# A fused attention and token-mixing kernel: units in pairs, quarter-array matmuls, word-wide f16 copies, stores held back

## The chip, the core and the metric

The kernel runs on one core of a Trainium2 chip. Times are device microseconds of one execution. The core has a matrix engine (TensorE, PE in the profile, with its weight loads listed apart as PEld), a vector engine (VectorE, DVE), an activation engine (ScalarE, ACT), a general engine (GpSimd, POOL) and a synchronisation engine (SyncE, SP). Each works through its own queue in order; they meet in semaphores. TensorE writes its results to PSUM, which has 8 banks of 2 KB in each of 128 partitions; VectorE and ScalarE bring them from there to the main on-chip memory (SBUF). Here POOL starts all loads and SP all stores, and 16 DMA engines carry them.

## The reference

Attention inside chunks of 64 tokens, for 8 batches, 8 heads, 576 tokens and 64 numbers a head, and after it, per batch, a token mixer without a softmax:

```python
scores = scale * np.matmul(q_c, k_c.transpose(0, 1, 2, 4, 3))    # per chunk of 64
scores = scores - np.max(scores, axis=-1, keepdims=True)
attn = np.exp(scores)
attn = attn / (np.sum(attn, axis=-1, keepdims=True) + 1e-09)
out = np.matmul(attn, v_c)
# the heads side by side give x: (8, 576, 512); then
wq = x @ w_q                                    # 512 -> 64
wk = x @ w_k
W_tok = scale * np.einsum('bsd,btd->bst', wq, wk)
mixed = np.einsum('bst,btd->bsd', W_tok, x)
return (np.maximum(mixed, 0.0) @ w_out).astype(np.float32)
```

Since nothing nonlinear stands between `W_tok` and `mixed`, the kernels form G = wk^T x first (64 x 512 for a batch) and then `mixed` = wq G.

## The kernel before, in words

**Units.** A unit is 128 tokens of one batch, all 8 heads: two chunks. 576 tokens are four units and 64 tokens over; the left-over tokens of two neighbouring batches make up one "rest" unit. Two batches are thus nine units, 36 in all.

**Loads.** POOL issues them in the order of the units (lines 197 to 212), casting fp32 to f16 on the way. q and k come for two units at a time, with two neighbouring tokens in one partition (line 176); v comes for one unit (line 195). Nothing is reused among these buffers, so no load waits for compute. The weights follow after the third and the fifth unit.

**Stages.** For two units the q and k tiles are turned by matmuls against the identity, with half the array's columns each ("tall", `turn`, line 233), and copied out of PSUM by VectorE (line 314). Then, unit by unit: scores, 16 matmuls of 64x64 in the two diagonal quarters of the array (line 336); their maximum and the subtraction on VectorE (lines 346 and 360); exp on ScalarE (370); the turn of the exponentials by the whole array or its column halves (230, 233) and its copy by ScalarE (381); the product with v and a column of ones, again in the two diagonal quarters (393); the denominators, their reciprocals and the division on VectorE (405 to 408). For two units together: the turn of x (230), its copy by ScalarE (441), the projections (448, 457) and their copy (467). For each batch: G in column halves (493, 502) and its copy (512). Then for two units the mixing in row halves (531) into two banks, the scaled ReLU by ScalarE bank by bank (551), by VectorE for one bank in the last two batches (549), and unit by unit the output product, 4 matmuls of 128x512 (567), its copy (577) and the store on SP (579), at once when the copy is done.

**Order.** Every such step is a `Node` with an engine, a priority, a cost and the nodes that it needs. `plan` (line 41) simulates the four queues before anything is emitted: at each turn it takes, among the nodes of an engine that could start within 0.25 us of the soonest, the one of least priority number (the unit's number plus a lag of the stage, line 277). A change of the array's form (full, tall, wide, quart) counts 0.094 us there. Of the 8 PSUM banks six go round singly and two are held together for the product with v. The engine of each step is fixed beforehand. The instructions are emitted in that order, and each engine runs its own in it.

Of the kernel before, what the change touches and what calls it, by code (L numbers as in the profile page):

```python
# [18 lines left out]
class Node:  # L19


    def __init__(self, eng, prio, busy, emit, deps, forms=(), takes=None, reads=None, tail=0.1):
        self.eng, self.prio, self.busy, self.emit = eng, prio, busy, emit
        self.deps, self.forms, self.tail = deps, forms, tail
        self.form = None
        self.takes = takes or []
        self.reads = reads
        self.done = None
        if reads is not None:
            reads.readers += 1  # L30


class Bank:


    def __init__(self, wide=False):
        self.wide, self.readers = wide, 0
        self.slot, self.left, self.tile, self.end = None, None, None, 0.0


def plan(nodes, ring, wides, switch=0.094, sem=0.06, look=0.25):


    free_at = {("r", i): 0.0 for i in range(ring)} | {("w", i): 0.0 for i in range(wides)}
    held = set()
    users = {}
    waiting = {}
    for n in nodes:
        waiting[n] = len(n.deps)
        for d in n.deps:  # L50
            users.setdefault(d, []).append(n)
    ready = {e: [] for e in ("PE", "DVE", "ACT", "DMA")}
    clock = dict.fromkeys(ready, 0.0)
    form = None
    for n in nodes:
        if not waiting[n]:
            ready[n.eng].append(n)
    order, left = [], len(nodes)

    def start_of(n):  # L60
        at = max([clock[n.eng]] + [d.done + sem for d in n.deps])
        slots = []
        for bk in n.takes:
            kind = "w" if bk.wide else "r"
            free = [(t, k) for k, t in free_at.items() if k[0] == kind and k not in held and k not in slots]
            if not free:
                return None, None
            early = [f for f in free if f[0] + sem <= at]
            t, slot = min(early, key=lambda f: (-f[0], f[1])) if early else min(free)
            at = max(at, t + sem)  # L70
            slots.append(slot)
        if n.eng == "PE" and form is not None and form not in n.forms:
            at = max(at, clock["PE"] + switch)
        return at, slots

    while left:
        best = None
        for e in ready:
            options = []
            for n in ready[e]:  # L80
                at, slot = start_of(n)
                if at is not None:
                    options.append((at, n.prio, n, slot))
            if not options:
                continue
            soonest = min(o[0] for o in options)
            o = min((o for o in options if o[0] <= soonest + look), key=lambda o: (o[1], o[0]))
            if best is None or o[0] < best[0]:
                best = o
        at, _, n, slot = best  # L90
        for bk, sl in zip(n.takes, slot):
            bk.slot, bk.left = sl, bk.readers
            held.add(sl)
        if n.eng == "PE":
            if form not in n.forms:
                form = n.forms[0]
            n.form = form
        clock[n.eng] = at + n.busy
        n.done = at + n.busy + n.tail
        n.at = at  # L100
        if n.reads is not None:
            n.reads.left -= 1
            n.reads.end = max(n.reads.end, n.done)
            if not n.reads.left:
                held.discard(n.reads.slot)
                free_at[n.reads.slot] = n.reads.end
        ready[n.eng].remove(n)
        for u in users.get(n, ()):
            waiting[u] -= 1
            if not waiting[u]:  # L110
                ready[u.eng].append(u)
        order.append(n)
        left -= 1
    return order


@with_exitstack
def kernel(
# [14 lines left out]
    CH, P, R, G = 64, 128, 2, 32  # L133
    NF = DM // P
    NM = S // P
    scale_attn = 1.0 / math.sqrt(D)
    scale_moe = 1.0 / math.sqrt(DH)
    VW = D + 2

# [5 lines left out]


    units, tiles = [], {}
    for b in range(0, B, 2):
        for bb, ms in ((b, range(NM)), (b, [None]), (b + 1, range(NM))):
            for m in ms:  # L150
                units.append((bb, m))
    NU = len(units)

# [6 lines left out]


    def rows(x, b, t0, n):
        return x[b, :, t0 : t0 + n, :].rearrange("h p d -> p h d")

    def pairs(x, b, t0, h0, h1):
        return x[b, h0:h1, t0 : t0 + 2 * P, :].rearrange("h (p r) d -> p h (r d)", r=R)

    qk = {}

    def load_pair(u, heads):  # L170
        b, m = units[u]
        for name, x in (("q", q), ("k", k)):
            qk[name, u] = const.tile([P, H, R * D], F16, name=f"{name}n{u}")
        for h0, h1 in heads:
            for name, x in (("q", q), ("k", k)):
                nc.gpsimd.dma_start(qk[name, u][:, h0:h1, :], pairs(x, b, m * P, h0, h1))  # L176

    def load_rest(u):
        b, _ = units[u]
        for name, x in (("q", q), ("k", k)):  # L180
            qk[name, u] = const.tile([P, H, D], F16, name=f"{name}n{u}")
            for i in range(2):
                nc.gpsimd.dma_start(
                    qk[name, u][CH * i : CH * i + CH, :, :], rows(x, b + i, NM * P, CH)
                )

    def load_v(u):
        b, m = units[u]
        if m is None:
            for i in range(2):  # L190
                nc.gpsimd.dma_start(
                    v_all[CH * i : CH * i + CH, u, :, 0:D], rows(v, b + i, NM * P, CH)
                )
        else:
            nc.gpsimd.dma_start(v_all[:, u, :, 0:D], rows(v, b, m * P, P))  # L195

    for u in range(NU):
        b, m = units[u]
        if m is None:
            load_rest(u)  # L200
        elif m % 2 == 0:
            load_pair(u, [(0, 4), (4, 8)] if u == 0 else [(0, 8)])
# [3 lines left out]
        if u == 2:  # L206
# [4 lines left out]
        if u == 4:  # L211
            nc.gpsimd.dma_start(wo[:], moe_w_out.rearrange("(f p) n -> p f n", p=P))

# [8 lines left out]
    PEd, DVd, ACd = 0.18, 0.09, 0.1  # L222
    FULL, TALL, WIDE, QUART = ("full",), ("tall",), ("wide",), ("quart",)
    EITHER = FULL + TALL

    def turn(form, to, of, i):


        if form == "full":
            nc.tensor.transpose(to, of[:, 2 * i : 2 * i + 2, :], ident[:])  # L230
        else:
            for o in range(2):
                nc.tensor.transpose(to[CH * o : CH * o + CH], of[:, 2 * i + o, :], ident[:])  # L233

    def dve(n, two=1):
        return n / two / 960 + 0.066
# [4 lines left out]
    def bank(tile_of, slot_of):  # L241

        shape, dtype, name = tile_of
        if slot_of.tile is None:
            kind, i = slot_of.slot
            slot_of.tile = psum.tile(shape, dtype, name=name, tag=f"{kind}{i}")
        return slot_of.tile

    arrive = {}
    at = 4.5  # L250
    for u in range(NU):
        b, m = units[u]
        if m is None:
            at += 0.75
        elif m % 2 == 0:
            at += 2.6
            arrive["v", u] = at
        arrive["qk", u] = at
        at += 0.7
        arrive["v", u] = at  # L260

    def landed(key):
        n = Node("DMA", 0, 0.0, lambda: None, [], tail=arrive[key])
        nodes.append(n)
        return n

    PU = 2 * NM + 1
    xs = {}

    def x_of(u):  # L270

        if u // PU not in xs:
            xs[u // PU] = work.tile([P, PU, H, D], F16, name="xs", tag="xs", bufs=2)
        return xs[u // PU][:, u % PU]

    st = {}
    LAG = {"tq": -3.0, "S": 0.0, "mx": 0.0, "E": 1.0, "PV": 1.0, "x": 1.0, "xT": 2.0, "pj": 2.0}

    def transposes(u):

        b, m = units[u]
        pri = u + LAG["tq"]
        there = landed(("qk", u))
        if m is None:
            bk = Bank()

            def pe(form):
                tp = bank(([P, 2, NF, P], F16, "tp"), bk)
                for t, name in enumerate("qk"):
                    for j in range(NF):  # L290
                        turn(form, tp[:, t, j, :], qk[name, u], j)

# [10 lines left out]
        for t, name in enumerate("qk"):  # L303
            bk = Bank()

            def pe(form, bk=bk, name=name):
                tp = bank(([P, NF, 4, R, G], F16, "tp"), bk)
                for j in range(NF):
                    for r in range(R):
                        turn(form, tp[:, j, :, r, :], qk[name, u][:, :, r * D : r * D + D], j)  # L310
# [340 lines left out]
```

## Time and profile before

| | |
|---|---|
| median of 3 runs | 164.35 us (164.33 to 166.39) |
| span of the profiled execution | 163.6 us |
| PE busy | 133.3 us, 81%, 2576 matmuls |
| DVE busy | 111.3 us, 68%, 227 instructions |
| ACT busy | 103.1 us, 63%, 187 instructions |
| POOL busy | 77.4 us, 47% |
| read from and written to memory | 29.75 MB, 9.44 MB |
| granted TensorE clock, mean | 0.986 |

The profiled execution's span runs from its first instruction to its last; the median of the runs is 0.7 us above it. A line of a group or a timeline names the source line, the engine, the operation, the result and its inputs, their shapes (partitions x elements) and a count, then microseconds. Busy time counts a matmul until its result is out, so that matmuls which follow each other overlap in it; how often one can start is read from the starts. The 40 digits of a slice row are tenths of 1/40 of the span. In a table of stretches each engine has its busy time and its number of instructions, then the granted clock, the DMA share and GB/s.

### The profile page before, as it was taken

The page shows a single profiled execution, that of the slowest core. Times are in us where ns is not written, and L with a number is a line of the kernel's source. Part 1 is how long each engine was busy: PE and PEld are TensorE (multiplying, and loading weights), DVE is VectorE, ACT ScalarE, POOL GpSimd, SP SyncE. Part 2 cuts the span into 40 slices and gives each one's busy share as a digit, 9 for nine tenths or more (in the row PEclk, how much of TensorE's full clock was granted, in tenths as well). Part 3 has the DMA queues.
Part 4 walks back from the last instruction along what each step waited for, and adds up shares of the span by engine and source line. Part 5 has one row for each costly group of instructions (what it writes and reads, how often), then busy time and mean ns, then how long its engine had stood idle before and what let it go on. Part 6 is the DMA issues. An engine that isn't in the chain of part 4 may idle for free.

```text
span 163.6 us, 5896 instructions
## 1 busy us (share of the span) xinstructions
PE 133.3 (81%) x2576; PEld 95.3 (58%) x2576; DVE 111.3 (68%) x227; ACT 103.1 (63%) x187; POOL 77.4 (47%) x100
## 2 busy tenths in 40 slices
PE   0447559798899989998999999989989997894870
PEld 0435448576557756775677667856766675553320
DVE  0164545979948947989499489985894899760350
ACT  3012023467798697878977968698779697944510
POOL 7999998674998445598672697000000000000000
PEclk9999999999999999999999999999999999999698
DMA  3999999999999999999999999993300422033053
GB/s 36 126 149 157 137 180 171 171 172 164 130 172 228 241 171 197 242 208 204 170 240 239 164 177 236 205 167 119 148 2 6 165 95 68 0 128 132 0 220 103
DMA packets 86650, 24.70 MB, mean 151 GB/s; under 512 B 81504, under 2 KB 82016, under 8 KB 86624
## 3 DMA queue, kind: packets, MB, share of 16 engines
q0 software_dynamic: 81376, 14.88, 112.2%
q1 hardware_dynamic: 5248, 9.44, 16.6%
q8 instruction: 20, 0.33, 0.8%
q14 instruction: 6, 0.05, 0.1%
HBM read 29.75 MB, written 9.44 MB: 240 GB/s over the span
## 4 chain that ended last, share of the span: by engine, by line
PE 39%; DVE 24%; ACT 15%; POOL 10%; DMA 4%; issue 4%; DVEq 0%; ACTq 0%; POOLq 0%
PE op L567 16%; DVE sh L360 8%; DVE mx L346 6%; DVE xs L408 5%; ACT rm L551 5%; PE xp L393 4%; DMA kn<-in_k_dram 4%; ACT es L370 4%; PE tp L233 3%; PE tx L230 3%; ACT xt L441 3%; PE sp L336 3%; PE pj L448 3%; POOL v_all L195 2%; POOL qn L176 2%
## 5 line engine op out<-in xcount | busy, mean ns | idle before, releaser
L567 PE MATMUL op<-wo,rm 128*128 128x512 f16 x144 | 37.8, 392 | 0.5 <-DVE rm L549 0.5
L370 ACT ACTIVATE es<-sh 128x512 f16<-128x512 f32 x36 | 23.2, 644 | 18.3 <-DVE sh L360 13.1
L381 ACT COPY et<-ep 128x512 f16<-128x512 f16 x36 | 21.7, 602 | 14.7 <-PE ep L233 9.4
L195 POOL DMA_DIRECT2D v_all<-in_v_dram x32 | 28.6, 912 | 1.9 <-DMA v_all<-in_v_dram 1.8
L346 DVE TENSOR_REDUCE mx<-sp 128x8 f32<-128x512 f32 x36 | 24.6, 682 | 2.6 <-PE sp L336 2.5
L408 DVE TENSOR_TENSOR xs<-xp,rec 128x512 f16<-128x512 f32 x36 | 24.9, 691 | 1.2
L577 ACT COPY osb<-op 128x512 f32<-128x512 f32 x31 | 19.0, 612 | 8.0 <-PE op L567 6.7
L360 DVE TENSOR_TENSOR sh<-sp,mx 128x512 f32<-128x512 f32 x32 | 22.1, 689 | 2.6 <-ACT xt L441 0.5
L314 DVE COPY qt<-tp 128x1024 f16<-128x1024 f16 x16 | 11.0, 685 | 16.5 <-PE tp L233 16.5
L551 ACT ACTIVATE rm<-ma 128x512 f16<-128x512 f32 (+1 forms) x35 | 20.3, 683 | 1.4 <-PE ma L531 1.4
L567 PEld LDWEIGHTS <-rm 128*128 128x128 f16 x144 | 13.2, 100 | 13.1 <-issue 2.2
L441 ACT COPY xt<-tx 128x1024 f16<-128x1024 f16 (+1 forms) x20 | 18.7, 934 | 2.7 <-PE tx L230 2.1
L233 PE MATMUL tp<-ident,qn 128*64 128x128 f16 x256 | 11.7, 239 | 9.9 <-POOL ident masks.py:199 5.0
L393 PE MATMUL xp<-v_all,et 64*64 64x65 f16 x576 | 16.8, 198 | 2.2 <-ACT et L381 0.7
L393 PEld LDWEIGHTS <-et 64*64 64x64 f16 x576 | 12.7, 110 | 9.3 <-ACT et L381 6.2
L176 POOL DMA_DIRECT2D kn<-in_k_dram x17 | 15.1, 886 | 5.5 <-DMA kn<-in_k_dram 4.5
L176 POOL DMA_DIRECT2D qn<-in_q_dram x17 | 15.3, 901 | 2.6 <-DMA qn<-in_q_dram 1.1
L314 DVE COPY kt<-tp 128x1024 f16<-128x1024 f16 x16 | 10.9, 683 | 6.5 <-PE tp L233 6.5
L233 PEld LDWEIGHTS <-qn 128*64 128x64 f16 x256 | 8.8, 120 | 11.1 <-DMA qn<-in_q_dram 9.9
L336 PE MATMUL sp<-kt,qt 64*64 64x64 f16 x512 | 13.2, 202 | 0.8 <-DVE kt L314 0.8
L230 PE MATMUL tx<-ident,xs 128*128 128x128 f16 x128 | 9.9, 219 | 4.6 <-ACT rm L551 3.7
L336 PEld LDWEIGHTS <-qt 64*64 64x64 f16 x512 | 11.0, 117 | 2.9 <-issue 1.8
(47 smaller groups left out, 178.8 us busy)
## 6 DMA issues: line engine op xcount, KB each, us to landing
out_dram<-osb SPq DMA_DIRECT2D x32, 256.0 KB, 4.2
v_all<-in_v_dram POOLq DMA_DIRECT2D x32, 128.0 KB, 9.1
qn<-in_q_dram POOLq DMA_DIRECT2D x15, 256.0 KB, 7.9
kn<-in_k_dram POOLq DMA_DIRECT2D x15, 256.0 KB, 8.5
out_dram<-osb SPq DMA_DIRECT2D x8, 128.0 KB, 3.8
qn<-in_q_dram POOLq DMA_DIRECT2D x8, 64.0 KB, 8.4
kn<-in_k_dram POOLq DMA_DIRECT2D x8, 64.0 KB, 6.5
v_all<-in_v_dram POOLq DMA_DIRECT2D x8, 64.0 KB, 4.8
```

What stands on the lines that cost most here:

```text
L176: nc.gpsimd.dma_start(qk[name, u][:, h0:h1, :], pairs(x, b, m * P, h0, h1))
L195: nc.gpsimd.dma_start(v_all[:, u, :, 0:D], rows(v, b, m * P, P))
L233: nc.tensor.transpose(to[CH * o : CH * o + CH], of[:, 2 * i + o, :], ident[:])
L336: nc.tensor.matmul(sp[r, 2 * j + c, :], lhsT=qt[r, j, c * CH : c * CH + CH], rhs=kt[r, j, c * CH : c * CH + CH], start=True, stop=True,)
L346: nc.vector.tensor_reduce(mx[:], bs.tile[:], axis=AX.X, op=ALU.max)
L360: nc.vector.tensor_tensor(out=sh[:].rearrange("p i (g r) -> p i r g", r=R), in0=sp[:].rearrange("p i (r g) -> p i r g", r=R), in1=mx[:, :, ...
L370: nc.scalar.activation(es[:], st["sh", u][:], AF.Exp, scale=scale_attn)
L393: nc.tensor.matmul(xv[r, h // 4, h % 4, :], lhsT=et[r, j, CH * hp : CH * hp + CH], rhs=v_all[r, u, h, 0 : D + 1], start=True, stop=True,)
L408: nc.vector.tensor_tensor(out=x_of(u).rearrange("p (w i) d -> p w i d", w=2), in0=xv[:, :, :, 0:D], in1=rec[:, :, :, None].broadcast_to([P ...
L441: nc.scalar.copy(xt[:], bt.tile[:])
L551: nc.scalar.activation(to, of, AF.Relu, scale=scale_moe)
L567: nc.tensor.matmul(op[:], lhsT=st[key][:, f, c0 : c0 + P], rhs=wo[:, f, :], start=(f == 0), stop=(f == NF - 1),)
```

## The change

- **Pairs.** q, k, scores, exponentials, v product, x, projection, mixing and output are all done for two units at a time (a rest unit is alone). Vector steps that took one bank (512 fp32) take two (1024): maximum, subtraction, exp, ReLU.
- **Quarters.** All work whose contraction is 64 deep (turns of q, k, the exponentials and x, scores, v product, mixing) goes as 64x64 matmuls in all four quarters of the array, and their results to the bank of their row half or crosswise (`half(c ^ i)`), where they were in halves, in the full array or in two quarters. Projections and output may go in full or tall form, G in tall form.
- **PSUM** is one tile of 8 banks; `plan` gives steps one bank or an aligned pair.
- **Copies** of f16 out of PSUM (qkt, et, xt) read and write the same bytes as half as many 32-bit words.
- **Engine.** Copies and ReLU have a cost on ACT and on DVE, and `plan` takes whichever would finish first. The lags and the look-ahead are other numbers; the arrival times of loads are modelled anew.
- **Loads.** q and k are one transfer each for a pair (the first pair too), the weights follow after the second and the fourth pair. The q/k tiles and the output tiles share 18 buffers.
- **Stores.** The first thing on SP is a 4-byte transfer out of the place where the last v load lands, so that all stores, behind it in the same queue, start after that load.

The diff, cut to its core:

```diff
-def plan(nodes, ring, wides, switch=0.094, sem=0.06, look=0.25):
+def plan(nodes, look, switch=0.094, sem=0.06, banks=8):
...
+        for n in ready:
+            there = max([d.done + sem for d in n.deps], default=0.0)
+            pick = None
+            for e, cost in n.cost.items():
+                at = max(clock[e], there)
+                if e == "PE" and form is not None and form not in n.forms:
+                    at = max(at, clock[e] + switch)
+                if pick is None or at + cost < pick[0]:
+                    pick = (at + cost, at, e)
...
+LAG = {"tq": -0.89, "S": -0.59, "E": -1.07, "V": -4.51, "x": -9.8, "xT": 3.13, "pj": -1.08, "G": -10.02, "mix": 0.16, "out": 2.78}
+LOOK = 0.223
...
+    ps = psum.tile([P, 8, 512], F32, name="ps")
...
+    def in_banks(bk, words, dtype=F32):
+        a = ps[:, bk.at : bk.at + bk.n, 0:words]
+        return a.bitcast(F16) if dtype == F16 else a
...
+    def either(n):
+        return {"ACT": act(n), "DVE": vec(n)}
+
+    def quart(n, cols):
+        return {"PE": n / 4 * (cols / 2400 + 0.0045)}
...
+            for t in range(2):
+                for j in range(HP):
+                    for r in range(1 if m is None else R):
+                        for i in range(2):
+                            for o in range(2):
+                                to = tp[half(o), i, t, j] if m is None else tp[half(o), i, t, j, :, r, :]
+                                of = qk[u][half(i), t, 2 * j + o, r * D : r * D + D]
+                                nc.tensor.transpose(to, of, ident[half(i), half(i)])
...
+                    copy(eng, tt[:].rearrange("p t j c s -> p (t j c s)").bitcast(F32), in_banks(bk, 512)[:, i])
...
-                for c in range(2):
-                    for hp in range(2):
-                        r = slice(CH * hp, CH * hp + CH)
-                        nc.tensor.matmul(
-                            sp[r, 2 * j + c, :],
-                            lhsT=qt[r, j, c * CH : c * CH + CH],
-                            rhs=kt[r, j, c * CH : c * CH + CH],
+            for i in range(ni):
+                for j in range(HP):
+                    for c in range(2):
+                        for o in range(2):
+                            nc.tensor.matmul(
+                                sp[half(c ^ i), o, i, j, :],
+                                lhsT=st["qkt", u, 0, i, j, c][half(o)],
+                                rhs=st["qkt", u, 1, i, j, c][half(o)],
...
+                            a = half(c ^ i)
+                            nc.tensor.transpose(ep[half(c), i, o, j, :], es[a, o, i, j, :], ident[a, a])
...
+                                nc.tensor.matmul(
+                                    to[half(c ^ i), i if ni == 2 else w, x, :],
+                                    lhsT=et[half(c), i, h % 2, h // 2, :],
+                                    rhs=v_all[half(c), first[u] + i, h, 0:W],
...
+                            of = xs[u][half(a), i, 2 * f + o, :]
+                            nc.tensor.transpose(tx[half(o), a, f, i, :], of, ident[half(a), half(a)])
...
+                            nc.tensor.matmul(
+                                ma[half(m2), o, f, s],
+                                lhsT=st["g", bb][half(o), f, half(m2)],
+                                rhs=st["wq", u][half(o), s],
...
+                if not held:
+                    held.append(const.tile([1, 2], F16, name="held"))
+                    nc.sync.dma_start(held[0][:], v_all[P - 1 : P, NU - 1, H - 1, D - 2 : D])
```

More of the change, by code (lines that the diff above doesn't have):

```diff
@@ L1 @@
-import heapq
 import math
@@ L29, in __init__ @@
         if reads is not None:
             reads.readers += 1
[L33 to L38, printed above, removed]
-def plan(nodes, ring, wides, switch=0.094, sem=0.06, look=0.25):
[L44 to L47, printed above, removed]
+class Banks:
+    def __init__(self, n):
+        self.n, self.readers, self.left, self.at, self.end = n, 0, 0, None, 0.0
@@ L48, in plan @@
+TAIL = {"PE": 0.17, "DVE": 0.09, "ACT": 0.1}
+def plan(nodes, look, switch=0.094, sem=0.06, banks=8):
+    free_at = [0.0] * banks
+    held = [False] * banks
+    users, waiting = {}, {}
     for n in nodes:
-        waiting[n] = len(n.deps)
+        waiting[n] = sum(d.done is None for d in n.deps)
         for d in n.deps:
             users.setdefault(d, []).append(n)
[L52 to L57, printed above, removed]
@@ L76, in plan @@
-    while left:
-        best = None
[L78 to L87, printed above, removed]
-            if best is None or o[0] < best[0]:
[L89 to L94, printed above, removed]
+    clock = dict.fromkeys(TAIL, 0.0)
@@ new lines, in plan, with place @@
+    ready = [n for n in nodes if n.cost and not waiting[n]]
+    form, order = None, []
+    def place(n, at):
+        taken, spots = set(), []
+        for bk in n.takes:
+            best = None
+            for i in range(0, banks, bk.n):
+                span = range(i, i + bk.n)
+                if any(held[x] or x in taken for x in span):
+                    continue
+                t = max(free_at[x] for x in span) + sem
+                buddy = i ^ 1
+                lone = bk.n == 1 and not held[buddy] and free_at[buddy] + sem <= at
+                key = (max(t, at), lone, -t, i)
+                if best is None or key < best[0]:
+                    best = (key, i)
+            if best is None:
+                return None, None
+            taken.update(range(best[1], best[1] + bk.n))
+            spots.append(best[1])
+            at = max(at, best[0][0])
+        return at, spots
@@ L97, in plan @@
             n.form = form
-        clock[n.eng] = at + n.busy
-        n.done = at + n.busy + n.tail
-        n.at = at
+        n.eng, n.start = e, at
+        clock[e] = at + n.cost[e]
+        n.done = clock[e] + TAIL[e]
         if n.reads is not None:
[L102 to L107, printed above, removed]
+            bk = n.reads
+            bk.left -= 1
+            bk.end = max(bk.end, n.done)
+            if not bk.left:
+                for x in range(bk.at, bk.at + bk.n):
+                    held[x], free_at[x] = False, bk.end
+        ready.remove(n)
         for u in users.get(n, ()):
@@ L203 @@
+    NBIG = NPB * B + 2
+    for u in range(len(pairs)):
+        load_qk(u)
         if u == 0:
@@ L220, in add, with landed @@
         return n
[L222 to L236, printed above, removed]
+    def landed(key):
+        n = add("dma", 0.0, {}, None, [])
+        n.done = arrive[key]
+        return n
@@ new lines, in mixing, with mix_out, pe @@
+        st["g_n", b] = add("g16", pri, either(2 * P), ev_g, [n], reads=bg)
+        for m, u in enumerate(mine):
+            mix_out(u, [b], at + LAG["mix"] + 0.5 * m, at + LAG["out"] + 0.5 * m)
+        if b % 2:
+            mix_out(rest, [b - 1, b], at + LAG["mix"] + 1.0, at + LAG["out"] + 1.0)
+    def mix_out(u, batches, pri, pri_out):
+        b, m = pairs[u]
+        ni = 1 if m is None else 2
+        toks = ni * P
+        bm = Banks(2)
+        osb = []
+        def pe(form):
+            ma = in_banks(bm, 2 * toks).rearrange("p o (f s) -> p o f s", f=2)
+            wide = toks // len(batches)
+            for f in range(2):
+                for i, bb in enumerate(batches):
+                    s = slice(i * wide, i * wide + wide)
+                    for m2 in range(2):
@@ L624 @@
+    for u, (b, m) in enumerate(pairs):
+        made = turns(u)
+        attention(u, made)
+        project(u)
+        if b % 2 == 0 and m is None or b % 2 == 1 and m == NPB - 1:
+            mixing(b, u)
+    for n in plan(nodes, LOOK):
+        n.emit(n.form if n.eng == "PE" else n.eng)
 _INS = ['q', 'k', 'v', 'moe_w_q', 'moe_w_k', 'moe_w_out']
```

655 lines of the change are left out of this document (296 added, 359 removed).

## The prediction

> **What bounds the kernel now.** I read the totals and the slices first, then the busy time of whole stretches, then single groups in time order. The page:
>
> ```profile
> span 163.6 us, 5896 instructions
> ...
> PE 133.3 (81%) x2576; PEld 95.3 (58%) x2576; DVE 111.3 (68%) x227; ACT 103.1 (63%) x187; POOL 77.4 (47%) x100
> ...
> PE   0447559798899989998999999989989997894870
> ...
> DMA  3999999999999999999999999993300422033053
> GB/s 36 126 149 157 137 180 171 171 172 164 130 172 228 241 171 197 242 208 204 170 240 239 164 177 236 205 167 119 148 2 6 165 95 68 0 128 132 0 220 103
> ...
> q0 software_dynamic: 81376, 14.88, 112.2%
> q1 hardware_dynamic: 5248, 9.44, 16.6%
> ```
>
> A slice is 4.09 us. PE is full from slice 7 to slice 36; loading (q0) fills the DMA engines until slice 27, 113 us, and PE works on for 40 us after that, so loads don't set the end. The work repeats every two batches (8 units and one rest unit, a **block** below): in the chain the same piece, PE op L567, stands at 58.33, 90.93 and 123.50 us, a period of 32.6 us. Busy time in three stretches of about one period (length, then PE, PEld, DVE, ACT):
>
> ```profile
> 41.00:74.00 33.00, 31.20 (x636) 21.89 (x630) 26.19 (x55) 26.21 (x49) 24.22 (x30) 1.00 1.84 198
> 74.00:106.00 32.00, 30.63 (x646) 22.36 (x644) 25.87 (x54) 26.49 (x49) 19.07 (x24) 1.00 1.83 205
> 106.00:139.00 33.00, 30.27 (x610) 21.58 (x606) 26.18 (x56) 26.93 (x50) 0.00 (x0) 1.00 0.43 97
> ```
>
> PE is busy 94%, DVE and ACT 80%: PE bounds the repeated part, at full granted clock (the 1.00). Four periods are 130 us; the other 33 us are the start (few data there yet) and the end (139 to 164 us: DVE and ACT busy some 10 of 25 us).
>
> **What one step costs.** Durations overlap, so I take start to start, from the timelines (start, duration):
>
> ```profile
> 62.22 0.32 PE L336 MATMUL sp<-qkt 64*64 64x64 f16 x9
> ...
> 69.33 0.64 PE L233 MATMUL tp<-ident,qn 128*64 128x128 f16 x16
> 69.80 0.39 PE L233 MATMUL ep<-ident,es 128*64 128x128 f16 x8
> 70.02 0.61 PE L233 MATMUL tp<-ident,kn 128*64 128x128 f16 x16
> ...
> 77.78 1.02 PE L567 MATMUL op<-wo,rm 128*128 128x512 f16 x4
> 78.64 0.60 PE L448 MATMUL pj<-xt,wq 128*128 128x256 f16 x4
> 79.08 0.40 PE L457 MATMUL pj<-wk,xt 128*128 128x64 f16 x8
> ```
> ```profile
> 65.41 0.68 DVE L353 TENSOR_TENSOR sh<-sp,mx 128x512 f32<-128x512 f32 x1
> 66.01 0.68 DVE L314 COPY kt<-tp 128x1024 f16<-128x1024 f16 x1
> ```
> ```profile
> 67.13 1.02 ACT L441 COPY xt<-tx 128x1024 f16<-128x1024 f16 x1
> 68.03 0.60 ACT L381 COPY et<-ep 128x512 f16<-128x512 f16 x1
> 68.51 0.65 ACT L370 ACTIVATE es<-sh 128x512 f16<-128x512 f32 x1
> ```
>
> The first line is from a stretch cut at 62.36: nine score matmuls start in 0.14 us, 15.8 ns each, on two of the four 64x64 quarters, so one quarter takes a new matmul each 31.6 ns. Half-array transposes: 16 in 0.47 us, 8 in 0.22, so 28 ns. An output matmul: 0.86/4 = 216 ns. Projections: 0.43 us for four, 30 ns for each 64-wide one. A change of array form: the 0.32 us from one group of 16 quarter matmuls to the next form, less 0.25, gives about 0.09. DVE: 0.60 us for 512 fp32 words and for 1024 f16 alike; 8-wide den and rec 0.20 and 0.24. ACT: 0.90 for 1024, 0.48 for 512, so 0.82 ns an element; exp 0.53, rm 0.57.
>
> **PE, part by part** (per pair of units). Now: q/k transposes 32 x 28 = 0.90; scores 0.51; E turns 0.45; V 0.51; x turns 0.45; projection 0.67; mixing 0.22; output 8 x 216 = 1.73: 5.44. Block: 4 pairs 21.8, the rest unit 2.7, G 1.4: 25.9; the rows show 30.7, so 4.8 us go to some 50 form changes and group tails. After: 64 + 32 + 32 + 32 + 32 = 192 matmuls in four quarters. The trace has two column halves side by side (L233), two row halves (L531), two diagonal quarters (L336), never four. So the price lies between 31.6 ns (one at a time) and 7.9 (31.6/4). I take 7.9: within a pair of quarters the next starts at once, and the bank is chosen by row half, as with L531. That is 1.52 instead of 2.82. Projection 0.71 (narrower pieces), mixing 0.22 (four times two quarters instead of twice two halves, same columns), output 1.73: 4.18. Block: 16.7 + rest 2.1 + G 1.4 = 20.2. Nearly all stages now share the quarter form; left are pj, out and G, some 16 groups a block, each two changes at most: 0.5 to 3.0 us. **PE 22.5 us a block, not 30.7.**
>
> **DVE and ACT.** DVE alone, per pair: max and subtract over two banks 2 x 1.14 (0.60 plus 512 x 1.04 ns, the slope between the 8-wide and the 512-wide rows; bounds 1.12 to 1.20) instead of 4 x 0.60, x and its den/rec unchanged 2.08: 4.35; block 19.6 with the rest. ACT alone: exp 0.94. Either engine, priced on ACT: qkt 2 x 0.48 (was DVE, 2 x 0.60), et 0.48 (was 0.96), xt 0.48 (was 0.90), wt 0.37, rm 1.05, osb 0.95. Reading f16 as 32-bit words halves the step on ACT. On DVE it gives nothing, since 1024 f16 and 512 words both take 0.60. The Trainium skill (PSUM — Partial Sum Buffer, Specifications) gives DVE 0.52 ns per 2-byte element in its paired mode and 1.04 otherwise, which speaks against this part; the two rows agree with it, and only the ACT share keeps a gain. ACT's block: 4.3 + 19.9 = 24.1; moving 2.0 of it to DVE at 1.25 times the price levels both at **22.1 us a block, not 25.6 (DVE) and 24.6 (ACT)** by the same count.
>
> **Loads and stores.** Before the first store the slices show 171 GB/s of loads. By 49 us 7.2 of 14.9 MB are in (the first twelve slices x 4.09); the rest at 0.171 MB/us takes 45 us: with stores held the last load lands at about **94 us**, 21.5 us a block. The hold is a wait on SP: a small transfer out of the last v tile, ahead of all 40 stores. Behind it on SP stands nothing else; the output tiles wait in the ring shared with q/k (18 buffers, 16 + 20 uses), and only the nineteenth needs an early one stored. So nobody waits, but the stores now form a block at the end: 16.6% x 163.6 = 27 us if the queue is never empty. That is a floor: 94 + 27 + 2 = 123 us of span. POOL's load issues fall by two, their order past the identity and the weights is nearly the same, and the first data come as late: cost nothing, 1 us at most.
>
> **Sum.** Three engines at 22.1 to 22.5 us and loads at 21.5 are level; none can be busy 94% as PE is now, when the others cover for it. I take 24 us a block (93%), bounds 22.5 and 28 (80%, what DVE and ACT show now). Outside the blocks 33 us now: I take 30, since the start stays load-limited and the last evictions may go to either engine, while chains of pairs are longer. 4 x 24 + 30 = 126 span, plus 0.7 (median 164.35 against the profiled 163.6): **127 us**.
>
> **Rivals.**
> - *Stores decide.* If the block runs at 22.5 us, the compute ends at 120 and the held stores at 123; with faster transfers 117 to 122. For: 27 us of stores after 94. Chance 0.12.
> - *Coarse steps.* Pairs hold two banks at a time, so four slots serve S, E, V, q/k turns, x turns and mixing; an engine stalled on the head of its queue keeps the others waiting. 27 to 28.5 us a block: 134 to 147. For: DVE and ACT at 80% now. Against: the bank order is planned over all eight. Chance 0.22.
> - *Two quarters at a time.* 15.8 ns: 1.5 us more per pair, PE 29.3 a block, period 31: 4 x 31 + 30 = 154 (148 to 161). Chance 0.05.
> - *Slower: quarters take turns.* At 31.6 ns the 192 cost 6.07 us, 4.55 more per pair; PE 43 a block, period 45, 211 us. It decides against the change from 17.4 ns a matmul on, where PE's block is again 30.7. Against: 15.8 ns is already shown. The Trainium skill (TensorE: Matmul & The Clock Gate, section on the 56 ns gap) says starts never come closer than about 25 ns; by that it would be about 188 us. The nine starts in 0.14 us contradict it for different quarters. Chance 0.07, with any other stall of this size.
> - *The change does nothing net* (161 to 168): 0.03.
>
> **How the numbers follow.** Forecast 120 to 134: 0.51. Leaving out the two slow cases, the last one and the edges, 116 to 146 holds some 8 in 10. A change under 2% can't be told from none here. Faster 0.90, same 0.03, slower 0.07.
>
> **What the profile after would show.** Right: score groups of 32 in about 0.25 us; PE near 22 to 23 busy in a block; DVE and ACT level; the loads over by slice 30 of 40 (94 of 126), stores after it only. Wrong: quarter groups of 32 taking 0.5 us or more; PE, DVE and ACT all under 80% in mid-span; the span ending in a run of stores with idle engines (then the floor decides).

## The result, and the profile after

| | before | after |
|---|---|---|
| median of 5 runs each | 165.06 us (164.33 to 167.1) | **187.72 us** (187.29 to 191.93) |
| ratio, 95% interval | | **1.135** (1.126 to 1.143): slower |
| span of the profiled execution | 163.6 us | 190.2 us |
| matmuls; pieces of instructions fetched (q8) | 2576; 20 | 4248; 33 |

The profiled execution of the changed kernel is its longest one (191.93 us); the other four lie between 187.29 and 187.75. I had forecast 127 us, in a range of 116 to 146. The page after:

```profile
span 190.2 us, 9165 instructions
...
PE 126.6 (67%) x4248; PEld 85.9 (45%) x4248; DVE 97.7 (51%) x180; ACT 93.5 (49%) x150; POOL 76.3 (40%) x98
...
PE   0442736789263748738478875995589966968980
...
PEclk9999999999855666996955897599975999999997
DMA  3999999999999999999994950232000320350373
...
q8 instruction: 33, 0.54, 1.1%
...
PE 56%; issue 21%; ACT 11%; DVE 7%; DMA 3%; POOL 0%; ACTq 0%; DVEq 0%; POOLq 0%
```

and two lines of the page before that the prediction did not show:

```profile
q8 instruction: 20, 0.33, 0.8%
...
PE 39%; DVE 24%; ACT 15%; POOL 10%; DMA 4%; issue 4%; DVEq 0%; ACTq 0%; POOLq 0%
```

PE's row has holes of 2 to 5 tenths through the whole span, where before it stood at 9. Nobody else is full: DVE and ACT are at half. In the chain, "issue", time in which an engine waited for nothing that the profile shows, went from 4% of 163.6 us to 21% of 190.2 us, from 7 to 40 us. The clock row, all 9 before but near the end, has stretches of 5 (52 us at half clock on record, 6.5 before). And the queue that the first lines of a page are seldom read for, q8, carries 33 packets instead of 20, 16 KB in each (0.54 MB / 33). They are PE's own instructions: its matmuls and weight loads together, divided by 256, give 33.2 and 20.1.

The clock row reads too high at the start. The first record of the clock stands at 44.3 us (29.4 us in the kernel before), and where none stands the row shows 9. The output matmuls tell the real pace (start, duration, group):

```profile
41.08 3.48 PE L585 MATMUL ps<-wo,rm 128*128 128x512 f16 x8
44.49 0.45 PE L327 MATMUL ps<-qkt 64*64 64x64 f16 x32
44.87 1.90 PE L585 MATMUL ps<-wo,rm 128*128 128x512 f16 x8
46.70 0.48 PE L287 MATMUL ps<-ident,qk 64*64 64x64 f16 x36
```

Eight of them take 3.41 us from start to start, 426 ns each, and the next eight 1.83 us, 229 ns each. So PE ran at half speed until 44 us. In the kernel before they take 215 ns from the first one on, at 43.9 us.

Stretches of the changed kernel (length, busy time of PE, PEld, DVE, ACT and POOL with the instructions, clock, DMA share, GB/s):

```profile
12.00:53.00 41.00, 25.41 (x895) 18.87 (x894) 20.90 (x38) 16.48 (x26) 33.07 (x41) 0.98 1.88 155
53.00:100.00 47.00, 29.78 (x1023) 20.86 (x1023) 24.09 (x49) 20.63 (x33) 32.36 (x40) 0.72 1.94 157
100.00:144.00 44.00, 33.66 (x1232) 21.99 (x1236) 27.79 (x48) 24.67 (x42) 0.00 (x0) 0.81 0.31 111
144.00:190.00 46.00, 35.64 (x1006) 22.41 (x1006) 21.61 (x43) 29.80 (x48) 0.00 (x0) 0.95 0.30 106
```

A block has about 4248 / 4 = 1062 matmuls. While loads run, 1023 take 47 us: 49 us a block. After the loads 1232 take 44: 38 us. I had 24. The clock alone is not it: the 128 matmuls from 78.6 us on lie wholly at full clock (75.0 to 85.3 us) and are 3.1 us of array time by the prediction's prices, and they took 6.57 us.

**Where PE stops.** PE's timeline from 56 to 72 us (start, duration, group; in brackets the idle time before it and who ended it):

```profile
59.77 0.42 PE L452 MATMUL ps<-ident,xs 64*64 64x64 f16 x15 [2.77 <-issue]
59.96 0.66 PE L327 MATMUL ps<-qkt 64*64 64x64 f16 x32
60.87 1.01 PE L473 MATMUL ps<-xt,wq 128*128 128x128 f16 x12 [0.26 <-ACT xt L264]
61.70 0.61 PE L483 MATMUL ps<-wk,xt 128*128 128x64 f16 x8
62.24 0.64 PE L378 MATMUL ps<-ident,es 64*64 64x64 f16 x32
62.88 1.42 PE L516 MATMUL ps<-xs,wt 64*64 64x256 f16 x10
64.23 0.49 PE L407 MATMUL ps<-v_all,et 64*64 64x65 f16 x19
65.96 0.31 PE L407 MATMUL ps<-v_all,et 64*64 64x65 f16 x13 [1.25 <-issue]
66.09 0.44 PE L287 MATMUL ps<-ident,qk 64*64 64x64 f16 x32
66.34 0.42 PE L552 MATMUL ps<-wt,g 64*64 64x256 f16 x8
67.37 0.41 PE L552 MATMUL ps<-wt,g 64*64 64x256 f16 x8 [0.60 <-DVE xs L433]
67.97 0.50 PE L378 MATMUL ps<-ident,es 64*64 64x64 f16 x32 [0.19 <-DVE xs L433]
68.24 0.45 PE L552 MATMUL ps<-wt,g 64*64 64x64 f16 x16
68.59 0.43 PE L327 MATMUL ps<-qkt 64*64 64x64 f16 x16
69.19 0.27 PE L407 MATMUL ps<-v_all,et 64*64 64x65 f16 x3 [0.17 <-ACT et L264]
71.88 0.55 PE L407 MATMUL ps<-v_all,et 64*64 64x65 f16 x24 [2.43 <-issue]
```

The three stops put down to "issue" fall in the middle of groups (15 left of 32, 13 left of 32, 24 and more left), where no semaphore is waited for. Count the matmuls between them: 15+32+12+8+32+10+19 = **128**, and 13+32+8+8+32+16+16+3 = **128**. The stops stand at matmuls 991, 1119, 1247, 1375, 1503 and so on, 128 further each time (127 once, at 1630). A matmul goes with a weight load, so that is 256 instructions, one packet of q8. From the records of q8: after such a stop PE resumes, the next packet is fetched only 4.04 us later (median of 11 while loads run; 1.12 us, median of 10, after them), the fetch takes 0.96, and 1.45 us after its end PE resumes again. That is a turn-around of some 6.4 us under load and 3.5 without; under load the first term varies from 1.7 to 4.3 us. Piece by piece (first matmul, when, array time of its 128 matmuls by the start-to-start prices of the prediction with 0.09 us for each change of form, what the piece took):

```
after    992   53.3   1.44   6.42        before    992   66.5   4.53   5.47
after   1120   59.8   2.37   6.20        before   1120   72.0   6.56   7.73
after   1248   66.0   1.32   5.92        before   1248   79.7   5.44   5.80
after   1376   71.9   3.88   6.75        before   1376   85.5   6.92   7.87
after   2656  126.7   1.01   3.64        before   1504   93.4   5.35   5.67
after   2784  130.4   1.77   3.45        before   2144  125.5   5.72   6.04
```

Before, 128 matmuls were 4.5 to 6.9 us of array time and took 0.3 to 1.2 us more: the fetch lay beside them. After, they are 1.0 to 4.7 us. While loads run, 12 of 15 pieces take 5.9 to 6.8 us whatever is in them (the others 4.3 to 5.4), and the light pieces after 120 us mostly 3.4 to 4.0. Summing the longer of turn-around and array time over all pieces gives an estimate of 167 us; with 12 us of start and some 6 of tail 185, against a span of 190.2. Direct stops for a fetch are 21, 38.7 us in all from the last start before to the first after. Before there are at most 2, 2.9 us, and the trace puts both down to something else (a load and ACT).

The Trainium skill (Runtime: NRT & Kernel Launch, Instruction fetch mechanics) says that an engine's instructions come in blocks of 256, fetched over a queue of its own during the current block, and that this is mostly hidden. The size agrees; hidden it is in the kernel before, not here.

### The profile page after: what moved, and what is told of

The parts are those of the page before. It is cut to its first block, busy times and chain, and to the rows that moved or that the text cites. A ratio compares the mean times of both kernels' runs of the same rounds, so it can differ in the third digit from the quotient of the medians.

```text
span 190.2 us, 9165 instructions
## 1 busy us (share of the span) xinstructions
PE 126.6 (67%) x4248; PEld 85.9 (45%) x4248; DVE 97.7 (51%) x180; ACT 93.5 (49%) x150; POOL 76.3 (40%) x98
## 4 chain that ended last, share of the span: by engine, by line
PE 56%; issue 21%; ACT 11%; DVE 7%; DMA 3%; POOL 0%; ACTq 0%; DVEq 0%; POOLq 0%
PE ps L585 19%; PE ps L473 7%; PE ps L287 6%; PE ps L407 4%; PE ps L516 4%; PE ps L327 4%; PE ps L378 3%; ACT rm L572 3%; PE ps L452 3%; PE ps L483 3%; DMA qk<-in_k_dram 3%; DVE xs L433 2%; PE ps L552 2%; ACT qkt L264 2%; ACT xt L264 2%
## 5 line engine op out<-in xcount | busy, mean ns | idle before, releaser
L585 PE MATMUL ps<-wo,rm 128*128 128x512 f16 (+1 forms) x148 | 41.9, 438 | 1.2 <-ACT rm L572 1.2
L340 DVE TENSOR_REDUCE mx<-ps 128x16 f32<-128x1024 f32 (+1 forms) x20 | 22.3, 1113 | 20.9 <-PE ps L327 20.9
L264 ACT COPY osb<-ps 128x512 f32<-128x512 f32 x31 | 18.2, 587 | 23.0 <-PE ps L585 22.8
L287 PE MATMUL ps<-ident,qk 64*64 64x64 f16 x1152 | 17.5, 214 | 17.8 <-issue 6.9
L287 PEld LDWEIGHTS <-qk 64*64 64x64 f16 x1152 | 15.1, 126 | 22.5 <-issue 14.2
L433 DVE TENSOR_TENSOR xs<-ps,rec 128x512 f16<-128x512 f32 x36 | 23.3, 682 | 0.2
L362 ACT ACTIVATE es<-sh 128x1024 f16<-128x1024 f32 (+1 forms) x20 | 19.4, 975 | 4.2 <-DVE sh L352 3.7
L264 ACT COPY qkt<-ps 128x512 f32<-128x512 f32 x26 | 14.5, 587 | 12.9 <-PE ps L287 12.6
L473 PE MATMUL ps<-xt,wq 128*128 128x64 f16 (+3 forms) x220 | 15.1, 228 | 7.9 <-issue 6.6
L572 ACT ACTIVATE rm<-ps 128x1024 f16<-128x1024 f32 (+1 forms) x14 | 16.5, 1208 | 7.0 <-PE ps L552 6.9
L352 DVE TENSOR_TENSOR sh<-ps,mx 128x1024 f32<-128x1024 f32 x16 | 19.5, 1222 | 0.4
L419 DVE TENSOR_SCALAR den<-ps 128x8 f32<-128x8 f32 x36 | 5.3, 164 | 22.1 <-PE ps L407 20.0
```

The costliest lines, as they stand in the source:

```text
L264: (nc.vector.tensor_copy if eng == "DVE" else nc.scalar.copy)(to, of)
L287: nc.tensor.transpose(to, of, ident[half(i), half(i)])
L340: nc.vector.tensor_reduce(mx[:], scores(), axis=AX.X, op=ALU.max)
L352: nc.vector.tensor_tensor(out=sh[:].rearrange("p x (g r) -> p x r g", r=R), in0=in_banks(bs, 512).rearrange("p o (x r g) -> p (o x) r g", ...
L362: nc.scalar.activation(es[:].rearrange("p o i j s -> p (o i j s)"), st["sh", u][:].rearrange("p x s -> p (x s)"), AF.Exp, scale=scale_attn,)
L433: nc.vector.tensor_tensor(out=to, in0=xp()[:, :, :, 0:D], in1=by, op=ALU.mult)
```

## The experiments

The theory is **F**: supply of PE's instructions, 128 matmuls in no less than the turn-around. Rivals: that time in the array sets the pace (**P**; the quarters' saving or their price), the order of the planned steps (**O**), the clock at half (**C**), the held stores.

**1. Fewer instructions.** The turns of q/k back in column halves, those of the exponentials and of x by the full array, scores still in four quarters (crossed by the head's half); 2752 matmuls, 21 pieces. Copies, pairs, hold and the two-bank vector steps are those of the change; the turns of exponentials and x need one bank a pair instead of two, and the order is planned anew.

```diff
-                        for i in range(2):
-                            for o in range(2):
-                                to = tp[half(o), i, t, j] if m is None else tp[half(o), i, t, j, :, r, :]
-                                of = qk[u][half(i), t, 2 * j + o, r * D : r * D + D]
-                                nc.tensor.transpose(to, of, ident[half(i), half(i)])
...
+                        for o in range(2):
+                            nc.tensor.transpose(to[half(o)], qk[u][:, t, 2 * j + o, r * D : r * D + D], ident[:])
...
-                            nc.tensor.transpose(ep[half(c), i, o, j, :], es[a, o, i, j, :], ident[a, a])
+                    nc.tensor.transpose(ep[:, i, j, :], es[:, i, j, :], ident[:])
...
-                                sp[half(c ^ i), o, i, j, :],
+                                sp[half(o ^ i), i, j, c, :],
```

> The changed kernel with fewer, larger turns: q and k in column halves (32 matmuls a pair for 64), exponentials and x by the whole array (8 each for 32), scores crossed by head instead of by chunk so that this fits; about 2750 matmuls for 4248, and more array time (about 0.8 us a pair). Pairs, two-bank steps, word copies, choice of engine and the held stores stay. Theory F: 21.5 pieces, some 14.5 of them until the loads end near 95 us, the rest at PE's own pace: 143 to 155 us. Rival O: the steps are as coarse, so 175 us or more. Rival P (array time decides, as the prediction had it): slower than the changed kernel by 16 us, 200 us or more.

160.39 us, ratio 0.974 (0.967 to 0.982). Fetch stops fall from 21 to 5, 7.1 us; half clock from 52 to 10 us. With more array time it is 27 us faster: P falls. O's 175 us falls too, though order and banks are not quite the same here; in run 3 they are. The time lies 5 us above F's range; run 5 below names the reason.

**2. More instructions.** Projections and output always in column halves: 4720 matmuls, 37 pieces.

```diff
-    QUART, TALL, EITHER = ("quart",), ("tall",), ("full", "tall")
+    QUART, TALL, EITHER = ("quart",), ("tall",), ("tall",)
```

> The changed kernel, but projections and output always in column halves (tall): the same array columns stream, in about 470 more matmuls (4248 to about 4720). Theory F (instruction supply): PE's instructions come in pieces of 256, that is 128 weight loads and matmuls; the next piece is asked for only when the last one is begun, and it takes 6.4 us while loads run and 3.7 us afterwards. 3.7 more pieces: 200 to 211 us. Rival C (the clock: small matmuls leave the array idle, so it is halved, and this is the loss): the array's work is the same, 184 to 191 us. Rival O (order: coarse steps of pairs): 184 to 191 us as well, less a little for fewer changes of form.

192.8 us, ratio 1.172 (1.162 to 1.182): 5 us more, not 12 to 23. The rough form of F, a fixed price for each piece, falls. Of the 472 added matmuls 332 are the projections' and 140 the output's; the fetch stops are 21 again, 41.6 us in all. The sum of the longer of turn-around and array time grows by some 11 us, which is still too much. The time lies 2 us above what C and O gave, nearer to them than to F, so this run does not decide between them.

**3. No loads beside the fetches.** Only the first pair and the first rest unit are loaded; everything later computes on these.

```diff
+        if u != like(u):
+            qk[u] = qk[like(u)]
...
+            return
```

> The changed kernel, same instructions on PE, ACT and DVE in the same order, but only the first pair and the first rest unit are loaded (and the weights); all later units compute on those. So the output is that of the first tokens, and loads load nothing after some 25 us. Theory F: without loads a piece takes 3.7 us, 33 pieces 123 us, so 127 to 142 us, and the waits of PE every 128 matmuls shrink from 2 to 3 us to under 1 us. Rival C: the quarter matmuls are the same, the clock halves as often, 175 us or more. Rival O: 175 us or more.

```profile
span 154.7 us, 9065 instructions
...
PE 112.7 (73%) x4248; PEld 79.4 (51%) x4248; DVE 97.1 (63%) x180; ACT 92.5 (60%) x150; POOL 11.4 (7%) x20
```

156.47 us (one run) with all 4248 matmuls in the same order, 31 us less: the same instructions in the same forms are not the price, and O falls. The wait for the next fetch is 1.12 us here at its first stop (at 40.6 us) as at the later ones, and light pieces come 3.72 us apart. Fetch stops fall by 25.8 us, to 12.9. The half clock on record falls as well, to 21.8 us, and its records begin at 25.7 us instead of 44.3: the clock did not halve as often, which C's 175 us had taken for granted. So this run does not exclude C by itself; that pieces at full clock take the turn-around too (78.6 us above) excludes it as the whole cause. My range was too low: it left out the 12 us of start, the tail, and the pieces with more array time than a turn-around (the longer of the two sums to 129 us; some 148 with start and tail). That PE is sooner at full speed and that loads no longer have to be waited for at all help too, and were not separated.

**4. Stores free.** The change without the hold.

```diff
-                if not held:
-                    held.append(const.tile([1, 2], F16, name="held"))
-                    nc.sync.dma_start(held[0][:], v_all[P - 1 : P, NU - 1, H - 1, D - 2 : D])
```

> The changed kernel without the held stores: each store starts when its tile is done. Theory F: loads last until 105 to 112 us instead of 95, so the slow turn-around lasts longer: 188 to 197 us. Rival S (the stores held to the end decide the time): 180 us or less.

188.63 us, ratio 1.148 (1.142 to 1.154). Loads end at 105.9 us instead of 99.2, the time is the same: "stores decide" falls for the kernel as changed.

**5. Fewer still, with and without the hold.** As run 1, and the product with v in two diagonal quarters without crossing, the projection whole, mixing in row halves: 2528 matmuls, 20 pieces; then the same without the hold (the three lines of run 4).

```diff
-                                    to[half(c ^ i), i if ni == 2 else w, x, :],
+                                    to[half(c), i if ni == 2 else w, x, :],
...
-                            nc.tensor.matmul(
-                                ma[half(m2), o, f, s],
-                                lhsT=st["g", bb][half(o), f, half(m2)],
...
+                        nc.tensor.matmul(
+                            ma[:, o, f, s],
+                            lhsT=st["g", bb][half(o), f, :],
```

> The kernel with the larger turns, and fewer matmuls still: the v product uncrossed, in two diagonal quarters, so that the projection needs 12 matmuls a pair for 20, and mixing in row halves, 4 for 8. About 2530 matmuls for 2752, with 0.2 us a pair more array time. Theory F: 1.75 pieces less, 150 to 158 us. Rival P (array time decides): 163 us or more.

> The kernel with the fewest matmuls (163.2 us with held stores), without the hold. With the hold its ScalarE waits 12.8 us for the first store (the ring of 18 buffers gives an output tile the buffer that came free first, and the eighth tile gets the first one's). If that wait is on the path: 148 to 156 us. If the stores among the loads cost as much as the wait did: 160 to 166 us.

With the hold 163.21 us, ratio 0.982 (0.973 to 0.991), a miss, and within what P gave; without it **154.71 us, ratio 0.938 (0.920 to 0.957)**, as expected and faster than both kernels. ACT's timeline with the hold:

```profile
86.92 2.46 ACT L548 ACTIVATE rm<-ps 128x1024 f16<-128x1024 f32 x2 [0.58 <-PE ps L528]
102.14 1.07 ACT L264 COPY osb<-ps 128x512 f32<-128x512 f32 x2 [12.76 <-DMA out_dram<-osb]
```

and SP's:

```profile
98.12 0.73 SPq L575 DMA_DIRECT2D held<-v_all  x1
98.91 4.86 SPq L581 DMA_DIRECT2D out_dram<-osb  x8
```

ACT stands 12.8 us for an output tile whose store may only start at 98.9 us, PE idles behind it. It is the eighth output tile: a new tile takes the place in the ring that came free first, and the first output tile's is that place. In run 1 the same wait is 6.7 us, about the size of its miss; in the change itself it costs nothing, since the slow kernel comes to that tile after 98 us. The page of the version without the hold:

```profile
span 152.2 us, 5726 instructions
...
PE 125.5 (83%) x2528; PEld 89.7 (59%) x2528; DVE 99.6 (65%) x182; ACT 91.6 (60%) x148; POOL 76.2 (50%) x98
```

PE's array time, an estimate by the prediction's prices with 0.09 us for each change of form, is 109 us, 22 more than in the change (87) and 6 less than before (115); so the 33 us by which this version beats the change are not array time, and P falls again. Fetch stops are 3, 4.7 us.

**6. One stage alone.** The fast version of run 5, with only the turns of x in four quarters again: 432 matmuls more (2960, 23 pieces), 3.4 us less array time.

```diff
-                    nc.tensor.transpose(tx[:, f, i, :], xs[u][:, i, 2 * f : 2 * f + 2, :], ident[:])
+                    for a in range(2):
+                        for o in range(2):
+                            of = xs[u][half(a), i, 2 * f + o, :]
+                            nc.tensor.transpose(tx[half(o), a, f, i, :], of, ident[half(a), half(a)])
```

> One stage alone: the kernel with the fewest matmuls and free stores (154.7 us), with the turns of x in four quarters again, as in the changed kernel: 32 matmuls a pair for 8, 16 for 4 in the rest unit, 432 more in all (2960 for 2528), 4 us less array time in all by the 0.45 and 0.25 us a pair. Theory F: 3.4 more pieces, some of them hidden behind long matmuls: 158 to 168 us. Rival P (array time decides): 149 to 153 us.

171.08 us, ratio 1.032 (1.020 to 1.044): **16 us slower**, a little above F's range, and the other way than array time. PE's timeline:

```profile
64.42 0.22 PE L438 MATMUL ps<-ident,xs 64*64 64x64 f16 x4 [1.04 <-issue]
64.57 1.08 PE L289 MATMUL ps<-ident,qk 128*64 128x128 f16 x32
65.58 0.45 PE L317 MATMUL ps<-qkt 64*64 64x64 f16 x32
65.96 0.61 PE L457 MATMUL ps<-xt,wq 128*128 128x256 f16 x4
66.41 0.40 PE L467 MATMUL ps<-wk,xt 128*128 128x64 f16 x8
66.64 0.61 PE L364 MATMUL ps<-ident,es 128*128 128x128 f16 x8
67.18 0.45 PE L438 MATMUL ps<-ident,xs 64*64 64x64 f16 x32
67.86 0.26 PE L317 MATMUL ps<-qkt 64*64 64x64 f16 x8 [0.23 <-ACT qkt L264]
71.16 0.53 PE L317 MATMUL ps<-qkt 64*64 64x64 f16 x24 [3.05 <-issue]
```

4+32+32+4+8+8+32+8 = 128 again: 3.5 us of work, then 3.05 us of nothing in the middle of a group. Fetch stops are 14.0 us (4.7 without), half clock 27 us (12). The order was planned anew with it and x takes two banks, so not all of the 16 us need be the fetch.

**7. Loads held back.** GpSimd starts a load only when the third last (in the last run: fifth last) has landed, so that fewer lie ahead of a fetch; with the change itself, with run 5 with the hold, and without it.

```diff
+        if n >= 3:
+            p, old = paced[n - 3]
+            nc.gpsimd.tensor_copy(pace[p : p + 1, n : n + 1], old)
+        nc.gpsimd.dma_start(to, rows)
```

> The changed kernel, with at most three loads in flight: before each load POOL reads one element of the load three earlier, and so waits for it (about six are in flight now: 7 us from issue to landing at 1.2 us each). Everything else stays. Theory F with a queue (the next piece of instructions waits behind the loads in flight, 4 us of the 6.4): the wait falls to about 2 us, a piece takes 4.5 us while loads run, 160 to 175 us in all. If the 4 us are not a matter of how many loads are in flight: 185 to 195 us, a little later for the later loads.

> The kernel with the fewest matmuls, with at most three loads in flight. Theory F with a queue: 3 to 8 us less than without the pacing. If the wait is not a matter of the loads in flight: 0 to 6 us more, for the later loads.

> The kernel with the fewest matmuls and free stores (154.7 us), with at most five loads in flight. With three, the wait for the next piece of instructions fell from 4.0 to 2.7 us, but loading took 45 us longer. With five: the wait some 3.5 us, loading a little longer. If the wait is worth more than the later loads: 150 to 153 us; if not: 156 to 166 us.

220.05 us (1.327; 1.312 to 1.342), 203.93 us (1.228; 1.212 to 1.243) and 160.98 us (158.26 to 162.14): all slower than without, the first two far outside both of their forecasts. With three loads in flight the median wait for a fetch falls from 4.04 to 2.72 us in the changed kernel (single waits from 1.1 to 3.7), the way the theory has it, but the last load lands at 143 and 138 us, and with the hold that is also when stores may begin (39 us of ACT's waits in the first). These two tell nothing of F in time. With five in flight and no hold, loads end at 122.4 us instead of 108.7 and the gain does not come; the wait for a fetch has two values there, too few to go by. That the 4 us are a backlog of loads fits two runs (1.12 with none, 2.72 with three in flight), but is not shown.

**8. An order that knows the supply.** The fast version of run 5, with 6.4 us (3.7 after 104 us) for each 128 matmuls in the planner, and lags chosen by that.

```diff
+            if c % 128 == 0:
+                b = max(t, b + (SLOW if b < LOADED else FAST))
+                t = b
```

> The same without the hold, and the order is planned with the instruction supply in it: in the plan PE may begin its next 128 matmuls no sooner than 6.4 us after it began the last 128 (3.7 us after 104 us of the plan's time), and the stage lags are chosen anew for that. Theory F: the order that spreads small and large matmuls evenly loses less to the supply, 141 to 150 us. If the order is not what matters: as without it, within 2%.

153.84 us (151.31 to 154.45), against 154.71 (153.92 to 159.72) without: F's 141 to 150 us is missed, and there is no gain that these runs can measure, though the mean clock is 0.995. With 20 pieces there is perhaps little left to plan around.

## Why the prediction was wrong, step by step

- **"I take 7.9" (four quarters at once): right.** At 106.56 and 106.84 us two groups start, 32 score matmuls apart: 8.75 ns each. So neither 31.6 nor 15.8 ns. Nor does the 25 ns of the Trainium skill (TensorE: Matmul & The Clock Gate, section on the 56 ns gap) hold across quarters; that the time came out at the 188 us which that rule gave is chance, since the loss is elsewhere.

```profile
106.56 0.45 PE L327 MATMUL ps<-qkt 64*64 64x64 f16 x32
106.84 0.44 PE L287 MATMUL ps<-ident,qk 64*64 64x64 f16 x32
```

- **"PE 22.5 us a block, not 30.7": the step that failed.** As array time it holds: by the prediction's prices 87 us over the kernel, some 22 a block, against 115 before, with 83 changes of form instead of 143. But I priced matmuls by their columns and never by their number. A block went from 644 to 1062 of them, 5.0 to 8.3 pieces; at 5.9 to 6.75 us a piece that is 49 to 56 us under load, where 49 was measured. Before, 5.0 pieces at 6.4 us are 32.2, and the period was 32.6: the supply was hidden, but with little room, so more matmuls with less array time each had to run into it. The packets stood in the page before (20 of q8), and its waits had an "issue" entry; I read neither.
- **"I take 24 us a block (93%)", and the full clock that goes with it.** The clock fell to half for 52 us on record, and PE was at half speed until 44 us besides. Five of the six recorded stretches inside the work begin during a fetch stop of 1.3 us or more or up to 2.1 us after it (at 51.1, 85.3, 95.5, 116.0 and 139.9 us). The sixth, at 68.2 us, begins 2.2 us after one of 1.25. Three stops of 1.5 to 1.8 us, at 130.4, 157.5 and 171.1 us, were followed by none. That stops bring the half clock is therefore likely, but not shown. With fewer stops there is less of it: 10 us with 2752 matmuls, 22 without the loads, where all the quarters are still there. How many of the lost microseconds are due to the clock alone was not separated; an output product of four took 1.82 us from its start to the next one's at half clock (100.95 to 102.77), 0.86 before.
- **"Level at 22.1 us" (DVE, ACT): right in size, worthless here.** Their busy time fell by 23.2 us together (214.4 to 191.2); 4 blocks of 6.0 were predicted. A word copy on ACT starts the next 0.47 us later (108.11 to 108.58), predicted 0.48. These parts are still in the version of 154.71 us. It also keeps the scores in four quarters, which adds no matmul and saves an estimated 4.6 us of array time (576 at 7.9 ns for 15.8), and it has 127 changes of form for 143; what each of these gained was not separated.
- **"So nobody waits ... only the nineteenth needs an early one stored": wrong.** It is the eighth, by the order of release. No cost in the change, 6.7 and 12.8 us once the rest is faster.
- **Loads at about 94 us: 99.2.** Loads weren't the bound. *Stores decide* and *two quarters at a time* didn't happen; *coarse steps* is not the cause, as run 3 has the same steps in the same order at 156 us. The slower rival had the right sign with the wrong mechanism, and I gave it 0.07, "with any other stall of this size".
- **The signs named:** score groups of 0.28 us came true and did not save the forecast; "PE, DVE and ACT all under 80% in mid-span" was the sign of wrong, and it is what the stretches show.

## What to carry to other kernels

Before splitting matmuls into smaller parallel ones, count PE's instructions: divide their number by 256, and compare the array time of 128 matmuls with the turn-around that the trace shows between two packets of the instruction queue (here 6.4 us beside heavy loads, 3.5 without). Stops in the middle of a group, put down to "issue" and a fixed number of matmuls apart, are its signature. Read PE's pace from the starts of one shape, since the clock row shows 9 where no record of the clock stands. Here the way out was to keep pairs, word copies and two-bank steps, spend quarters only where they add no instructions, and let stores go at once.

## What was not expected of the hardware

- PE's instruction supply: 256 instructions a piece; resume to next fetch 4.04 us under loads, 1.12 us without, 0.96 us the fetch, 1.45 us from its end to the next matmul. So 128 matmuls mostly took no less than about 6.4 us (50 ns each) or 3.5 us (28 ns each), however short they were.
- Four quarters do run four at a time, at 8.75 ns a matmul, within a piece.
- PE stayed at half speed until 44 us in the change and until 29 us before; the half clock on record later was 52 us in the change, 27 us in the kernel with 432 more matmuls in one stage, 12 us in the same without them. It mostly began beside fetch stops of 1.3 us or more, but not every such stop brought it.
